# One image line loaded in two parts, a shorter second dummy product, and one warming instruction less, in an attention and gated feed-forward kernel

## The chip, the cores and the metric

The kernel runs on one core of a Trainium2 chip. The metric is the device time of one execution in microseconds (us). The engines are TensorE (PE in the profile; PEld is its weight load), VectorE (DVE), ScalarE (ACT), GpSimd (POOL) and SyncE (SP, which here only issues transfers). Sixteen DMA engines move the data; SP, ScalarE and GpSimd each have a queue of transfers that they issue (SPq, ACTq, POOLq).

## The reference

An attention over a pooled image, followed by a gated feed-forward layer. With four images (B = 4), 12288 queries for each, and 128 channels:

```
# q [4, 12288, 128], kv [4, 384, 32, 128], w_sr [128, 128]
kv_pool = kv.reshape(B, H // r, r, W // r, r, C).mean(axis=(2, 4))      # r = 4: 96 x 8 = 768 keys
k = v = kv_pool.reshape(B, -1, C) @ w_sr
a = softmax(q @ k.T / sqrt(C))
x = (a @ v).reshape(B * 12288, 128)
gate = maximum(x @ w_gate, 0.0)                                       # w_gate, w_val [128, 1536]
out = (gate * (x @ w_val)) @ w_out                                    # w_out [1536, 128]
```

All inputs and the output are float32.

## The kernel before

The queries are worked in 96 tiles of 512 rows (`T`), four to a group. For a tile, TensorE makes the scores against the 768 keys, ScalarE the exponentials, TensorE the weighted values, and then for each of twelve blocks of 128 hidden units a value product (line 504), a gate product (515) and, after VectorE has put the two together (523), an output product (545 or 529). The order in which all engines get these steps is written out by hand: a list of words `OPENING` for the first tiles, then `STEADY` for each tile, and `DRAIN` and `LAST` for the end. Each word is one step; `@n` behind it names the PSUM bank.

The change touches the very beginning. An image is pooled in six chunks of 128 keys. Two chunks are one pair, 128 image rows. `kv_load` brings a pair in as four "lines": line `dh` holds the rows `dh`, `dh`+4, `dh`+8 and so on. One line is a tile of 128 partitions with 1024 float32 each, 512 KB. Its source has 32 image rows ("hp"), and each row is cut into four pieces of 4 KB ("wp"), so that four neighbouring partitions hold one image row. For the first pair of the first image the lines go to two queues in turn:

```
kv_load(0, 0, range(r), (nc.sync, nc.scalar))
nc.sync.dma_start(w_sr_f32, w_sr)
q_load_pair(0)
q_load_pair(2)
kv_load(0, 1)
kv_load(0, 2)
```

So SP issues lines 0 and 2, then `w_sr` (line 642), two query pairs of 512 KB (line 181), and four lines each for the next two pairs (line 246; the last four are called `kv_line` in the profile). ScalarE issues lines 1 and 3, then loads its table, and runs two one-column exponentials, `warm` (line 651) and `spare` (652), whose results nothing reads.

TensorE begins with two dummy products, `fill(2)` (line 663), of the float32 identity matrix with a broadcast column of 512; their PSUM bank is given back at once. Then follows the start of `OPENING`:

```
T0.1@0 T1.1@1 T0.0 T1.0 T0.3 a1 T0.2 p1 kvT0 r1 cast0 pj0@0 T1.r cast1 qt0@2 key0 kvT1
```

- `Tj.d` (`turn_add`, line 300): four transposing matmuls that add the four pixel columns of line `d` of chunk `j` into a PSUM bank. The first one, `T0.1`, reads line 1.
- `a1`, `p1` and `r1` (line 272): chunk 1's lines 2 and 3 are added by VectorE, then the pixel columns by VectorE and GpSimd; `T1.r` transposes the result.
- `kvT0`, `kvT1` (line 143): VectorE copies the transposed chunk out of PSUM; `pj0` (line 314) multiplies it by `w_sr`, and `key0` (323) keeps the keys.
- `cast0`, `cast1`, `cast2` (line 141): ScalarE casts query tiles to float16 as soon as they have landed; `qt0` (line 209) transposes a tile on TensorE, `qT0` (143) copies it out, and `S` (378) are the scores.

The framework gives the transfers that SP and ScalarE issue eight semaphores in turn, in the order of the program. A transfer that takes a semaphore anew is issued only after the transfer that had it before, eight places back, has landed. The first such wait before the change stands at the second load of pair 1.

Of the kernel before, what the change touches and what calls it, by code (L numbers as in the profile page):

```python
# [11 lines left out]
AF = mybir.ActivationFunctionType  # L12
# [4 lines left out]
def kernel(  # L17
# [23 lines left out]
    nc = tc.nc  # L41

    B, N, C = q.shape
    _, H, W, _ = kv.shape
# [13 lines left out]
    X_SCALE = 512.0  # L58
    LEAD = GRP
    AT_BUFS = 4  # L60
    qk_scale = 1.0 / math.sqrt(C)

    assert C == 128 and N % T == 0 and J == 128 * NJC and D_FF == 128 * NFB
# [58 lines left out]
    def bank(shape, dtype=FP32):  # L122
        n = asked.pop() if asked else next(n for n in free_banks if n < usable[0])
        free_banks.remove(n)
        ps = pools[n // 6].tile(shape, dtype, tag=f"bank{n}", bufs=1, name="bank_ps")
        bank_numbers[id(ps)] = n, ps
        return ps
# [3 lines left out]
    def freed(ps):  # L131
        free_banks.append(bank_numbers.pop(id(ps))[0])
        return ps
# [95 lines left out]
    def kv_load(b, pair, lines=range(r), queues=(nc.sync,)):  # L229
        if (b, pair) not in kv_in:  # L230
            if (b, pair) == (0, NJC // 2 - 1):
                kv_in[b, pair] = [
                    work.tile([128, NS * J // 2], FP32, tag="a16", bufs=4, name="kv_line")[
                        :, 0 : 2 * r * C
                    ].rearrange("p (h dw c) -> p h dw c", h=2, dw=r)
                    for dh in range(r)
                ]
            else:
                lines_in = work.tile([128, r, 2, r, C], FP32, tag="kv_in", bufs=2, name="kv_in")
                kv_in[b, pair] = [lines_in[:, dh] for dh in range(r)]  # L240
        parts = kv_in[b, pair]
        rows = kv[b, pair * 2 * HC : (pair + 1) * 2 * HC].rearrange(
            "(hp dh) (wp h dw) c -> dh hp wp (h dw c)", dh=r, h=2, dw=r
        )
        for dh in lines:
            queues[dh % len(queues)].dma_start(  # L246
                parts[dh].rearrange("p h dw c -> p (h dw c)"), rows[dh]
            )

    s3s, kv_Ts, key_banks = {}, {}, {}  # L250

# [122 lines left out]
    def scores(k, jc):  # L374
        if k not in aTs:
            aTs[k] = work.tile([128, NJC, T], FP16, tag="aT", bufs=AT_BUFS, name="aT")
        s_ps = s_banks[k, jc] = bank([128, T])
# [9 lines left out]
    def score_block(k, s):  # L387
        b = k // NST
        if s == 0:
            a16s[k] = work.tile([128, NS, J], FP16, tag="a16", bufs=4, name="a16")  # L390
            aTs[k] = work.tile([128, NJC, T], FP16, tag="aT", bufs=AT_BUFS, name="aT")
            if k % 2 == 0:
# [238 lines left out]
    ident = const.tile([128, 128], FP32)  # L631
# [7 lines left out]

    w_sr_f32 = const.tile([128, C], FP32)  # L640
# [6 lines that stand above are left out]
    warm = const.tile([128, 1], FP32)  # L647
    spare = const.tile([128, 1], FP32)
    for tile_ in (spare, warm):
        nc.vector.memset(tile_, 0.0)  # L650
    nc.scalar.activation(warm, warm, AF.Exp)
    nc.scalar.activation(spare, spare, AF.Exp)

    wg16 = const.tile([128, D_FF], FP16)
    wv16 = const.tile([128, D_FF], FP16)
# [2 lines left out]

    idle = bank([128, 512])

    def fill(n):
        for _ in range(n):
            nc.tensor.matmul(
                idle, ident, ident[:, 0:1].to_broadcast([128, 512]), start=True, stop=True
            )

    fill(2)
    freed(idle)

    def fill_less(n):  # L670
# [135 lines left out]
    for word in OPENING:  # L806
        word, _, number = word.partition("@")
# [6 lines left out]
    for k in range(LEAD + 2, last + 1):  # L814
# [5 lines left out]
        b = k // NST + 1  # L820
# [3 lines left out]
        for word in words:  # L824
            head, n = word.rstrip("0123456789"), int(word.lstrip("abcdefghijklmnopqrstuvwxyzADPT") or 0)
# [29 lines left out]
            elif head in ("tb", "P", "pk"):  # L855
                pair, since = divmod(at - 6 if head == "tb" else at - 8, 4)
# [45 lines left out]
```

## Time and profile before

| | us |
|---|---|
| median of 3 runs | 1025.21 |
| lowest and highest | 1024.92, 1026.33 |
| the profiled execution | 1025.06 |
| its span, first to last instruction | 1023.3 |

| busy in the profiled span | us | share | instructions |
|---|---|---|---|
| TensorE matmul | 1016.5 | 99% | 5028 |
| TensorE weight load | 486.5 | 48% | 5028 |
| VectorE | 867.2 | 85% | 1447 |
| ScalarE | 918.3 | 90% | 1926 |
| GpSimd | 523.0 | 51% | 1311 |

The span is what the profiler saw of the instructions; the execution's own time is 1.76 us longer. A row of the timeline gives the start in us from the start of the span, the duration, the engine, the line of the kernel, the operation, what it writes and reads, how many instructions were merged, and in brackets the idle time before it with what ended it. A letter q behind an engine's name (SPq, ACTq) marks an instruction that issues a transfer; its duration is that of the issue, not of the transfer.

### The profile page before, as it was taken

The page shows a single profiled execution, that of the slowest core. Times are in us where ns is not written, and L with a number is a line of the kernel's source. Part 1 is how long each engine was busy: PE and PEld are TensorE (multiplying, and loading weights), DVE is VectorE, ACT ScalarE, POOL GpSimd, SP SyncE. Part 2 cuts the span into 40 slices and gives each one's busy share as a digit, 9 for nine tenths or more (in the row PEclk, how much of TensorE's full clock was granted, in tenths as well). Part 3 has the DMA queues.
Part 4 walks back from the last instruction along what each step waited for, and adds up shares of the span by engine and source line. Part 5 has one row for each costly group of instructions (what it writes and reads, how often), then busy time and mean ns, then how long its engine had stood idle before and what let it go on. Part 6 is the DMA issues. An engine that isn't in the chain of part 4 may idle for free.

```text
span 1023.3 us, 17491 instructions
## 1 busy us (share of the span) xinstructions
PE 1016.5 (99%) x5028; PEld 486.5 (48%) x5028; DVE 867.2 (85%) x1447; ACT 918.3 (90%) x1926; POOL 523.0 (51%) x1311
## 2 busy tenths in 40 slices
PE   8999999999999999999999999999999999999998
PEld 4444444444444444444444444444444444444445
DVE  4988888888888888888888888888888888888888
ACT  5999998999999999999999999989999999999986
POOL 3487857344347576544434856754434533443342
PEclk9999999999999999999999999999999999999999
DMA  9999998888799999768779989878777877777551
GB/s 316 167 170 184 194 201 146 140 126 125 139 196 157 199 168 181 137 116 144 124 132 204 172 172 196 159 125 137 128 132 113 147 122 129 124 119 124 98 91 44
DMA packets 475743, 153.48 MB, mean 150 GB/s; under 512 B 451584, under 2 KB 465920, under 8 KB 475648
## 3 DMA queue, kind: packets, MB, share of 16 engines
q1 hardware_dynamic: 453184, 126.08, 65.0%
q0 software_dynamic: 22032, 25.19, 18.0%
q10 hardware_dynamic: 432, 1.11, 0.3%
q8 instruction: 39, 0.64, 0.3%
q14 instruction: 56, 0.46, 0.2%
HBM read 53.94 MB, written 26.35 MB: 78 GB/s over the span
## 4 chain that ended last, share of the span: by engine, by line
PE 98%; DMA 1%; ACT 0%; SPq 0%; issue 0%
PE bank_ps L504 24%; PE bank_ps L515 24%; PE bank_ps L545 24%; PE wide_ps L397 12%; PE bank_ps L439 12%; DMA q<-in_q_dram 1%; PE bank_ps L529 1%; PE bank_ps L456 0%; PE bank_ps L378 0%; PE wide_ps L336 0%; PE bank_ps L300 0%; ACT aT L381 0%; PE bank_ps L314 0%; PE bank_ps L474 0%; SPq L246 0%
## 5 line engine op out<-in xcount | busy, mean ns | idle before, releaser
L523 DVE SCALAR_TENSOR_TENSOR hT<-bank_ps,val 128x512 f16<-128x512 f32 x1152 | 728.1, 680 | 104.5 <-PE bank_ps L515 83.8
L141 ACT CAST val<-bank_ps 128x512 f16<-128x512 f32 x1149 | 628.5, 596 | 44.6 <-PE bank_ps L504 24.2
L504 PE MATMUL bank_ps<-xT,wv 128*128 128x512 f16 x1152 | 420.6, 379 | 0.0
L515 PE MATMUL bank_ps<-xT,wg 128*128 128x512 f16 x1152 | 376.0, 379 | 0.0
L545 PE MATMUL bank_ps<-hT,wo 128*128 128x512 f16 x1116 | 348.5, 379 | 0.0
L402 ACT ACTIVATE a<-wide_ps 128x768 f16<-128x768 f32 x368 | 302.1, 821 | 44.1 <-PE wide_ps L397 44.1
L397 PE MATMUL wide_ps<-kv,qT 128*128 128x512 f16 x736 | 179.7, 326 | 0.0
L439 PE MATMUL bank_ps<-aT,kv 128*128 128x512 f16 x552 | 178.9, 379 | 0.0
L558 POOL TENSOR_TENSOR o_sb<-o_t,scale 128x512 f32<-128x512 f32 x89 | 93.2, 1047 | 159.6 <-issue 141.9
L545 PEld LDWEIGHTS <-wo 128*128 128x128 f16 x1116 | 109.2, 98 | 132.1 <-issue 1.1
L515 PEld LDWEIGHTS <-wg 128*128 128x128 f16 x1152 | 112.7, 98 | 122.6 <-issue 0.6
L504 PEld LDWEIGHTS <-wv 128*128 128x128 f16 x1152 | 112.6, 98 | 105.3 <-issue 0.6
L423 POOL COPY scale<-square 32x8 f32<-32x8 f32 x736 | 141.2, 192 | 28.6
L416 POOL TENSOR_TENSOR square<-inverse 128x8 f32<-128x8 f32 x46 | 9.3, 202 | 247.8 <-DVE inverse L414 241.0
L832 POOL DMA_DIRECT2D out_dram<-o_sb x208 | 130.3, 632 | 9.2 <-POOL o_sb L558 7.5
L397 PEld LDWEIGHTS <-qT 128*128 128x128 f16 x736 | 72.0, 98 | 86.9 <-issue 0.2
L447 DVE CAST xT<-bank_ps 128x512 f16<-128x512 f32 x92 | 63.6, 691 | 31.6 <-PE bank_ps L439 31.6
L439 PEld LDWEIGHTS <-kv 128*128 128x128 f16 x552 | 54.0, 98 | 65.2
L402 ACT ACTIVATION_READ_ACCUMULATOR a<-wide_ps 128x1 f32 x368 | 76.1, 207 | 0.0
L553 DVE STREAM_TRANSPOSE o_t<-bank_ps 128x512 f32<-128x512 f32 x93 | 65.4, 703 | 0.2 <-PE bank_ps L504 0.2
L162 POOL DMA_DIRECT2D q<-in_q_dram x84 | 48.8, 582 | 0.3 <-issue 0.3
L256 POOL TENSOR_TENSOR s<-kv_in 128x512 f32<-128x512 f32 x36 | 45.1, 1283 | 0.7
(81 smaller groups left out, 206.2 us busy)
## 6 DMA issues: line engine op xcount, KB each, us to landing
kv_in<-in_kv_dram SPq DMA_DIRECT2D x42, 512.0 KB, 5.2
out_dram<-o_sb SPq DMA_DIRECT2D x177, 64.0 KB, 3.6
q<-in_q_dram POOLq DMA_DIRECT2D x88, 128.0 KB, 3.5
out_dram<-o_sb POOLq DMA_DIRECT2D x176, 64.0 KB, 4.2
aT<-a SPq DMA_TRANSPOSE x184, 4.5
kv_line<-in_kv_dram SPq DMA_DIRECT2D x4, 512.0 KB, 9.9
placed<-blocks SPq DMA_DIRECT2D x9, 128.0 KB, 2.6
kvT<-placed SPq DMA_DIRECT2D x36, 32.0 KB, 2.2
```

The lines of the kernel that those rows point to most:

```text
L141: nc.scalar.copy(to, what)
L397: nc.tensor.matmul(s_ps[:, j0 * 128 : j1 * 128], qT, kv16[:, b, j0:j1, 0:C], start=True, stop=True)
L402: nc.scalar.activation(a16s[k][:, s, :], s_banks.pop(s)[:, 0:J], AF.Exp, scale=qk_scale, accum_out=a_sums[k // 2][:, k % 2, s : s + 1],)
L423: nc.gpsimd.tensor_copy(to[32 * b : 32 * (b + 1), :, :, j], squares[k // 2][32 * j : 32 * (j + 1)])
L439: nc.tensor.matmul(x_banks[k], kv16[:, k // NST, jc, C : 2 * C], aT[:, jc], start=first, stop=x_left[k] == 0,)
L504: nc.tensor.matmul(proj_banks["v", k, fb], wv16[:, fb * 128 : (fb + 1) * 128], xTs[k], start=True, stop=True,)
L515: nc.tensor.matmul(proj_banks["g", k, fb], wg16[:, fb * 128 : (fb + 1) * 128], xTs[k], start=True, stop=True,)
L523: nc.vector.scalar_tensor_tensor(hTs[k][:, fb, :], freed(proj_banks.pop(("g", k, fb))), 0.0, vals.pop((k, fb)), op0=ALU.max, op1=ALU.mult,)
L545: nc.tensor.matmul(o_banks[k], wo16[:, fb, :], hTs[k][:, fb, :], start=first, stop=o_left[k] == 0)
L553: nc.vector.transpose(o_t, freed(o_banks.pop(k)))
L558: nc.gpsimd.tensor_tensor(to, o_by, scale.to_broadcast([128, NS, 4, 32]), op=ALU.mult)
L832: queue.dma_start(*out_moves.pop())
```

## The change

Three edits. In `kv_load`, line 1 of the first pair of the first image is loaded by two transfers, partitions 0 to 31 (8 image rows) and 32 to 127 (24 image rows), both on ScalarE's queue, ahead of line 3. All other lines are loaded by one transfer as before. The tile and its readers stay the same; a reader of line 1 now waits for both. The exponential of `spare` is left out; its memset stays. The second dummy product has 384 columns instead of 512.

```diff
+    FIRST_CUTS = (0, 32, 128)
...
         for dh in lines:
-            queues[dh % len(queues)].dma_start(
-                parts[dh].rearrange("p h dw c -> p (h dw c)"), rows[dh]
-            )
+            cuts = FIRST_CUTS if (b, pair, dh) == (0, 0, 1) else (0, 128)
+            for p0, p1 in zip(cuts, cuts[1:]):
+                queues[dh % len(queues)].dma_start(
+                    parts[dh][p0:p1].rearrange("p h dw c -> p (h dw c)"), rows[dh, p0 // 4 : p1 // 4]
+                )
...
     nc.scalar.activation(warm, warm, AF.Exp)
-    nc.scalar.activation(spare, spare, AF.Exp)
...
-    def fill(n):
-        for _ in range(n):
-            nc.tensor.matmul(
-                idle, ident, ident[:, 0:1].to_broadcast([128, 512]), start=True, stop=True
-            )
-
-    fill(2)
+    for n in (512, 384):
+        nc.tensor.matmul(
+            idle[:, 0:n], ident, ident[:, 0:1].to_broadcast([128, n]), start=True, stop=True
+        )
     freed(idle)
```

In the program that results, TensorE, VectorE, GpSimd and SP have the same instructions in the same order; ScalarE has one more transfer in front and one activation less. The one more transfer moves the rotation of the eight semaphores on by one, so that each later transfer of SP's opening waits for another one than before: the first load of pair 1 for the first part of line 1, the next for line 0, then the second part of line 1, line 2, line 3, `w_sr`, and the two query pairs.

## The prediction

> **What bounds the kernel now.** I read the page first: the busy row (TensorE 99% of the span), then part 4, the chain that ended last.
>
> ```profile
> PE 98%; DMA 1%; ACT 0%; SPq 0%; issue 0%
> ```
>
> The one percent that is not TensorE sits at the start, where all three edits lie. The chain in order of time shows it: from 3.07 to 10.59 us the end of the kernel hangs on the load of the first query pair, then on its cast by ScalarE, then TensorE has the chain to the end.
>
> ```profile
> 3.07 7.53 DMA q<-in_q_dram
> 10.59 0.02 issue
> 10.62 1.15 ACT q L141 x2
> 11.77 0.05 issue
> 11.81 0.40 PE bank_ps L209 x4
> ```
>
> Next the timeline of the first 11 us (start, duration, engine, line, operation, shapes, and in brackets the idle time before it with its releaser).
>
> ```profile
> 0.74 1.56 SPq L246 DMA_DIRECT2D kv_in<-in_kv_dram  x2
> 0.74 1.29 ACTq L246 DMA_DIRECT2D kv_in<-in_kv_dram  x2
> 1.36 3.78 PE L663 MATMUL bank_ps<-ident 128*128 128x512 f32 x4 [1.36 <-POOL ident masks.py:199]
> 2.06 1.28 ACT L651 ACT_TABLE_LOAD   x1 [2.06 <-issue]
> 3.47 0.19 ACT L652 ACTIVATE spare<-spare 128x1 f32<-128x1 f32 x1
> 5.46 2.40 PE L300 MATMUL bank_ps<-ident,kv_in 128*128 128x128 f32 x16 [0.31 <-DMA kv_in<-in_kv_dram]
> 8.69 1.16 PE L300 MATMUL bank_ps<-ident,kv_in 128*128 128x128 f32 x8 [0.83 <-DMA kv_in<-in_kv_dram]
> 9.25 0.69 DVE L272 TENSOR_TENSOR kv_s<-kv_in 128x512 f32<-128x512 f32 x1 [8.34 <-DMA kv_in<-in_kv_dram]
> 10.62 1.90 ACT L141 CAST q<-q 128x512 f16<-128x512 f32 x3 [6.96 <-DMA q<-in_q_dram]
> 10.65 0.49 PE L314 MATMUL bank_ps<-kvT_chunk,w_sr_f 128*128 128x128 f32 x2 [0.81 <-DVE kvT_chunk L143]
> ```
>
> Every engine waits for loads. Last, busy time by microsecond (the last two columns are the DMA share and GB/s) and the queues between 2 and 4 us (q10 is ScalarE's, q1 SP's):
>
> ```profile
> 2.00:3.00 1.00, 1.00 (x2) 0.34 (x1) 0.00 (x0) 0.94 (x1) 0.08 (x1) 1.00 0.87 127
> 3.00:4.00 1.00, 1.00 (x2) 0.34 (x1) 0.00 (x0) 0.65 (x3) 0.00 (x0) 1.00 0.80 274
> 4.00:5.00 1.00, 1.00 (x2) 0.00 (x0) 0.00 (x0) 0.00 (x0) 0.00 (x0) 1.00 0.98 401
> 5.00:6.00 1.00, 0.69 (x4) 0.57 (x4) 0.00 (x0) 0.00 (x0) 0.00 (x0) 1.00 1.04 422
> ```
> ```profile
> q10 hardware_dynamic: 98, 0.40, 83.5%
> ```
>
> From 4 us on the DMA engines are full at some 410 GB/s, so a 512 KB load costs about 1.28 us of all sixteen engines (0.16 us for each of the 8 packets of 4 KB that fall to one engine). Until 4 us only line 1, ScalarE's first load, moves: no q1 packet is in that stretch, though SP issued line 0 at the same 0.74 us. Issue plus time to landing puts line 1 at 5.3, line 0 at 6.5, line 3 at 8.6, line 2 at 9.2, the first queries at 10.6: one behind the other, about 1.3 us for each 512 KB. So what counts in the opening is the total of the packets ahead of the first queries on the slowest DMA engine; who is first matters less.
>
> **The change, part by part.**
>
> *Warming activation removed.* ScalarE loses 0.19 us at 3.47 us and then waits until 10.62 us for the queries (6.96 us idle). Gain nothing. The extra issue on its queue, 0.62 to 0.64 us by the two rows of L246, pushes the table load from 2.06 to about 2.7 us and its end to 4.0; the remaining warming instruction ends near 4.2. The same 6.96 us hide that; without them it would cost 0.64 us less 0.19.
>
> *Shorter second dummy.* Each product runs as two passes; the passes start about 0.85 us apart (3.78 us for four with the tail). 384 of 512 columns take a quarter from two passes: 2 x 0.21 = 0.43 us, so the dummy ends near 4.72 instead of 5.14. TensorE already waits 0.31 us after it for line 1, so this gains nothing; it makes the wait longer. Its possible price is a clock that comes up later, below.
>
> *Semaphore rotation.* Transfers take eight semaphores in turn, and an issue waits for the transfer eight places back. One more transfer moves each wait of SP by one place: the first load of image pair 1, issued at 4.44 us without a wait, now waits for the 32-partition part; the three behind it for line 0, the 96-partition part and line 2; the first `kv_line` load for line 3. Queued behind on SP are only later image loads, then the late query tiles, which wait for GpSimd until 22.13 us. The readers of these loads are TensorE (waits of 0.41 and 0.34 us) and VectorE (0.65 and 0.40). The cover: the last of these issues stands at 11.89 us, while the load issued at 4.44 lands at 13.1, so q1 never runs dry. Cost nothing; with the cover gone, at most the 0.6 us of one issue.
>
> *The split.* The bytes are the same. Order changes: the 96-partition part is now ScalarE's second issue at about 1.4 us, where line 3 stood, and so comes behind line 0. Line 0 then has a quarter of line 1 before it and lands about 3/4 x 1.28 = 0.96 us earlier, near 5.5; the 96-partition part shares the engines with line 2 as line 3 did (between 5.6 and 8 us q1 had 53% and q10 50%), and needs 0.96 us alone or 1.9 us shared: line 1 is whole at 6.5 to 7.4 us instead of 5.3. Line 3 becomes the third issue and lands among the last, near the 9.2 us that line 2 had. TensorE's list has line 1 first, so its 16 transposes start at 6.5 to 7.4; at 0.11 us each, as the later ones of them run, they end by 9.2. The eight for lines 3 and 2 then follow at once and end near the 10.3 us at which VectorE copies their sum now. This is just hidden; if not, each 0.1 us of lateness is 0.1 us for the key chain, which has about 0.16 us of slack against the queries.
>
> What remains is how the two parts are spread over the sixteen engines. The loads of the trace have 32 blocks of four rows (one image row is four partitions), two whole blocks to an engine if they are spread evenly. The parts have 8 and 24 blocks. No row shows such a transfer. Lower bound: spread evenly, 2 and 6 packets, 0. Upper bound: a block stays whole, so 8 blocks fill at most eight engines with 4 packets each, and 24 blocks load some engines with 8 packets: 12 instead of 8, which is 4 x 0.16 = 0.64 us more on those engines for every later load. A gain on this term is excluded for the loaded engines, but if the engine that ends last now is one that is spared, part is won back. I take 0.5, near the end that keeps blocks whole, since all loads shown have whole numbers of blocks per engine.
>
> The Trainium skill, page "DMA: Bandwidth & Descriptors", section "Why a DMA increments its semaphore by 16 and not by 1", says that a copy runs on the largest number of engines, at most 16, that divides the slowest dimension of both sides. By that rule the parts run on 8 and 12 engines, and the sum would be the upper bound, 0.64 us; no run shown here has such a transfer, so the trace neither agrees nor disagrees.
>
> *Sum.* Warming 0, dummy 0, rotation 0, order 0, spread +0.5 us on the landing of the first queries. From there the chain is TensorE to the end, so it is passed on whole. The profiled execution took 1025.06 us, 1.76 more than its span of 1023.3; with 0.5 it becomes 1025.6. It lies 0.15 under the median of the runs shown, 1025.21, and against that the forecast is 1025.7.
>
> **The rivals.**
>
> *Evenly spread, order alone:* 0 to 0.2 us, 1025.3. For it: sixteen arrivals per load in all rows; against: 8 blocks are fewer than sixteen engines.
>
> *Earlier data:* the small part reaches the DMA engines sooner, and the slow first stretch (127 and 274 GB/s) is covered. At most the 0.43 us by which the dummy was shortened could be used: 1024.8. Against it: an issue costs 0.62 to 0.64 us here, and 0.33 to 0.38 at the kernel's end for small stores, so most of it is fixed; the second part comes a whole issue later.
>
> *A cold TensorE* (the one on the slower side). The transposes show two speeds:
>
> ```profile
> L300 PE MATMUL bank_ps<-ident,kv_in 128*128 128x128 f32 x4 | 1.1, 428 | 0.3 <-DMA kv_in<-in_kv_dram 0.3
> L300 PE MATMUL bank_ps<-ident,kv_in 128*128 128x128 f32 x13 | 1.7, 287 | 0.0
> ```
>
> The first row is from 5.4 to 6.3 us, the second from 6.45 to 8 us: 0.21 us from start to start, then 0.11. The step comes after about 5 us of nearly unbroken work. With the dummy ending at 4.72 and line 1 at 6.5 to 7.4 there is a hole of 1.8 to 2.7 us instead of 0.31. If the 0.11 us spacing comes only at about 9.8 us, 16 transposes cost up to 16 x 0.1 = 1.6 us more, of which the waits of 0.83 and 0.81 us absorb most: about +0.5 on top, 1026.2. If it comes only at 13 us, the 2.3 us of work between 10.65 and 13 double as well: 0.5 + 0.5 + 2.3 = 3.3, 1028.5. It decides where the 0.21 us spacing reaches past some 12 us. Against it: the hole is short beside the work after it. The Trainium skill, page "TensorE: Matmul & The Clock Gate", section "Part 1: The HAM clock gate (the "warmup" mystery)", has the clock follow a free-running window of 3.4 us; the step after some 5 us agrees, and by it a half-idle window would delay the fast clock by one window, the 1026.2 case.
>
> *No effect at all* would need the parts to be merged again; the order of instructions shows both on ScalarE's queue, so it has no chance of its own.
>
> **How the numbers follow.** Spread over fewer engines, +0.5: 0.45. Even: 0.24. Earlier data: 0.12. Cold to 9.8 us: 0.10. Cold to 13 us: 0.09. A measurement of this kernel can tell about 0.2%, 2.05 us, from no change: 1023.2 to 1027.3. Only the last case passes it; with 0.03 from the upper tail of the others slower has 0.12. Faster would need more than TensorE's waits of 0.31, 0.83 and 0.81 us together, so 0.03; same 0.85. The range runs from the earlier-data case with the low side of the runs (0.3 under the median) to above the cold-to-9.8 case with the high side (1.1 above the median): 1024.5 to 1027.2.
>
> **What would show it.** Right: three ScalarE issues at about 0.74, 1.4 and 2.0 us; the dummy at 3.35 us; the first transposes at 6.5 to 7.4; the cast of the queries at 11.1 instead of 10.62, and the products after it shifted by the same. Fewer engines: the two landings of line 1 and all later loads late by up to 0.64 us. Wrong: queries at 10.6 or earlier, or transposes at 0.21 us beyond 9.8 us, or any stage after 30 us that takes longer than before, for which I have no cause.

## The result, and the profile after

The changed kernel took 1030.8 us (median of 6 runs, 1030.54 to 1031.41) against 1025.45 for the kernel before (6 runs, 1024.92 to 1026.33): a ratio of 1.0053, 95% interval 1.0042 to 1.0063. It is slower by 5.35 us and lies outside the forecast range, on the side that had 0.12. The profiled execution took 1030.61 us with a span of 1028.8, 5.5 more than before.

The shares of the chain that ended last, on the page of the changed kernel:

```profile
PE 98%; DMA 1%; issue 0%; ACTq 0%; ACT 0%; DVE 0%
```

The loss is again in the one percent at the start. Against the trace of before, each TensorE instruction compared with the same one there, they are 5.6 to 6.8 us late from the first transposes on and 5.6 us late from 18.9 us (24.5 in the changed kernel) to the end. The chain in order of time (start, duration, what):

```profile
0.74 1.45 ACTq L249
2.19 0.03 issue
2.22 8.81 DMA kv_in<-in_kv_dram
11.03 0.14 issue
11.17 5.07 PE bank_ps L303 x24
16.24 0.02 issue
16.27 0.30 DVE kvT_chunk L144
16.57 0.04 issue
16.61 0.49 PE bank_ps L317 x2
```

Where the chain ran over the queries, it now runs over ScalarE's two issues, the second of which (the 96-partition part) is whole only at 11.03 us, and then over all 24 transposes in one piece. The timeline of the opening, to be laid beside that of before:

```profile
0.74 2.98 ACTq L249 DMA_DIRECT2D kv_in<-in_kv_dram  x3
0.74 1.33 SPq L249 DMA_DIRECT2D kv_in<-in_kv_dram  x2
1.36 3.35 PE L664 MATMUL bank_ps<-ident 128*128 128x512 f32 x4 [1.36 <-POOL ident masks.py:199]
3.75 1.28 ACT L654 ACT_TABLE_LOAD   x1 [3.75 <-issue]
11.17 5.06 PE L303 MATMUL bank_ps<-ident,kv_in 128*128 128x128 f32 x24 [6.45 <-DMA kv_in<-in_kv_dram]
12.12 1.14 ACT L142 CAST q<-q 128x512 f16<-128x512 f32 x2 [6.88 <-DMA q<-in_q_dram]
13.60 0.69 DVE L275 TENSOR_TENSOR kv_s<-kv_in 128x512 f32<-128x512 f32 x1 [12.69 <-DMA kv_in<-in_kv_dram]
16.61 0.49 PE L317 MATMUL bank_ps<-kvT_chunk,w_sr_f 128*128 128x128 f32 x2 [0.38 <-DVE kvT_chunk L144]
```

The dummy ends at 4.71 us, as forecast. Then TensorE waits 6.45 us instead of 0.31. The 24 transposes stand 0.21 us apart, all but the last two (5.06 us; before, 16 took 2.40 and 8 took 1.16). VectorE's sum of lines 2 and 3 comes at 13.60 instead of 9.25, since line 3 is whole only at 13.50. The first projection stands at 16.61 instead of 10.65.

The minimum, median and maximum duration in ns of ScalarE's three issues, from the answer on that line:

```profile
L249 ACTq DMA_DIRECT2D kv_in<-in_kv_dram x3: 652/821/1451, 0.7 to 3.1; - x3
```

In order they are 1451 (32 partitions), 821 (96) and 652 (line 3). The queues between 2 and 4 us, and the busy time by microsecond (last two columns DMA share and GB/s):

```profile
q1 hardware_dynamic: 94, 0.39, 84.6%
```
```profile
4.00:5.00 1.00, 0.72 (x2) 0.00 (x0) 0.00 (x0) 1.00 (x1) 0.00 (x0) 1.00 1.03 401
6.00:7.00 1.00, 0.00 (x0) 0.00 (x0) 0.00 (x0) 0.00 (x0) 0.00 (x0) 1.00 0.98 300
8.00:9.00 1.00, 0.00 (x0) 0.00 (x0) 0.00 (x0) 0.00 (x0) 0.00 (x0) 1.00 1.04 250
9.00:10.00 1.00, 0.00 (x0) 0.00 (x0) 0.00 (x0) 0.00 (x0) 0.00 (x0) 1.00 1.02 238
11.00:12.00 1.00, 0.83 (x4) 0.86 (x5) 0.00 (x0) 0.00 (x0) 0.00 (x0) 1.00 1.04 418
```

The order has turned round: before, q10 (ScalarE's) alone had packets up to 4 us; now q1 alone has. And from 6 to 11 us, while the 96-partition part moves, the engines are as full as ever (0.97 to 1.06) but move 238 to 307 GB/s. The packets show why: those of 4 KB, on both queues, take 256 to 283 ns on average between 7 and 10 us; before they took 159. At 11 us, when the part is done, the old rate is back. The first part, of 32 partitions, shows none of this: from 4 to 5 us, while its packets moved, they took 161 ns on average and the rate was 401 GB/s.

The landings in the two traces:

| whole at (us) | line 1 | line 0 | line 2 | line 3 | first queries | second queries |
|---|---|---|---|---|---|---|
| before | 5.32 | 6.58 | 9.15 | 8.64 | 10.59 | 11.87 |
| changed | 5.47 and 11.03 | 5.16 | 6.72 | 13.50 | 12.10 | 13.70 |

### The profile page after: what moved, and what is told of

Read it like the earlier page. It is cut to its first block, busy times and chain, and to the rows that moved or that the text cites. A ratio compares the mean times of both kernels' runs of the same rounds, so it can differ in the third digit from the quotient of the medians.

```text
span 1028.8 us, 17491 instructions
## 1 busy us (share of the span) xinstructions
PE 1017.4 (99%) x5028; PEld 488.4 (47%) x5028; DVE 867.2 (84%) x1447; ACT 918.2 (89%) x1925; POOL 522.9 (51%) x1311
## 4 chain that ended last, share of the span: by engine, by line
PE 98%; DMA 1%; issue 0%; ACTq 0%; ACT 0%; DVE 0%
PE bank_ps L507 24%; PE bank_ps L518 24%; PE bank_ps L548 23%; PE wide_ps L400 12%; PE bank_ps L442 12%; DMA kv_in<-in_kv_dram 1%; PE bank_ps L303 1%; PE bank_ps L532 1%; PE bank_ps L381 1%; PE bank_ps L459 1%; PE wide_ps L339 0%; PE bank_ps L317 0%; PE bank_ps L477 0%; ACTq L249 0%; PE bank_ps L210 0%
```

## The experiments

Diffs are against the changed kernel. Kernels were timed beside runs of the kernel before on the same chip, whose medians were 1024.88 to 1025.72; the ratio is to these. "First projection" is TensorE's first instruction of L317, "last line" the time at which the last of lines 0 to 3 is whole.

### Which of the three edits

**No split**, the two small edits alone.

```diff
-    FIRST_CUTS = (0, 32, 128)
+    FIRST_CUTS = (0, 128)
```

> Line 1 in one transfer again, with the shorter dummy and without the second warming instruction. If the split makes the loss (by its engines or by its place in the queue), this is the kernel before: within 1 us of it, line 1 landing at 5.3 us, the first transposes at 5.4. If the shorter dummy makes it (TensorE stays at its 0.21 us spacing), the loss stays: 2 to 5 us slower than before, transposes at 0.21 us well past 8 us.

1025.07 us, ratio 1.0004 (0.9994 to 1.0013). Line 1 is whole at 5.22 us again. The shorter dummy and the dropped warming instruction cost nothing that these runs can tell. The profiled execution, 1026.33 us, is 1.3 above the median. In it the clock, the column before the DMA share, was half from 11.12 to 14.54 us, with this opening too; TensorE was level with the trace of before until 11 us and 1.2 us late at what stood at 14 us there.

```profile
12.00:13.00 1.00, 1.00 (x7) 0.74 (x5) 1.00 (x5) 0.40 (x1) 0.00 (x0) 0.50 1.05 418
```

**Split only**, with the old dummy and both warming instructions.

```diff
+    nc.scalar.activation(spare, spare, AF.Exp)
-    for n in (512, 384):
+    for n in (512, 512):
```

> The split alone, both dummy products of 512 columns and both warming instructions. If the split makes the loss: 5 to 6 us slower than before, line 1 whole at about 11 us, 24 transposes at 0.21 us. If the dummy makes it: within 1 us of the kernel before.

1031.34 us, 1.0061 (1.0044 to 1.0078): the whole loss. The first issue took 1.46 us, the second part was whole at 11.03, line 3 at 13.49, and the first projection came at 16.90.

### Is it a second transfer, its size, or its partitions

**Two halves.**

```diff
-    FIRST_CUTS = (0, 32, 128)
+    FIRST_CUTS = (0, 64, 128)
```

> The changed kernel with the cut at 64 partitions: two parts of 16 source blocks each. If it is the number of engines that a part gets (8 and 12 with 8 and 24 blocks), both parts now run on all sixteen: 16 arrivals each, ScalarE's issues back to 0.6 to 0.7 us, the DMA rate above 400 GB/s from 4 us on, line 1 whole at 6 to 7.5 us, and the time 0 to 2 us above the kernel before. If any second transfer on ScalarE's queue falls behind SP's loads, line 1 stays late, at 9 us or more, and the loss is 3 to 5 us.

1026.0 us, 1.0011 (1.0001 to 1.002). Sixteen arrivals for each half. The issues are normal:

```profile
L249 ACTq DMA_DIRECT2D kv_in<-in_kv_dram x3: 608/618/665, 0.7 to 2.1; - x3
```

ScalarE's data come first again, and the halves are whole at 4.68 and 7.03 us. But the rate dips here too, to 291 and 303 GB/s between 5 and 7 us (packets of 0.21 to 0.26 us). The queries come 0.42 us later than before. The clock was half from 7.73 to 11.14 us in this execution, so the lost microsecond cannot be put down to the rate alone.

**A quarter, a quarter, a half**, so that no part has 96 partitions.

```diff
-    FIRST_CUTS = (0, 32, 128)
+    FIRST_CUTS = (0, 32, 64, 128)
```

> The changed kernel with line 1 in three parts of 32, 32 and 64 partitions: 8, 8 and 16 blocks, so no part has 24. If the part on twelve engines makes the slow stretch from 6 to 11 us (DMA engines fully busy at 250 to 300 GB/s), the rate is above 380 GB/s there and line 1 is whole at 7 to 9 us: 1 to 4 us slower than before. If parts on eight engines do it as well, or the number of transfers counts, it is as slow as the changed kernel or slower: 5 to 7 us.

1030.52 us, 1.0051 (1.0036 to 1.0066). Nearly all the loss without the 96-partition part: the first issue takes 1.457 us again, the second of the same size only 0.70; parts are whole at 5.64, 8.20 and 10.16, line 3 at 12.66. So the 12-engine part alone is not the cause. Here too the second part of 32 partitions moved with packets of 0.16 us (between 6 and 7 us), and packets were slow while the contiguous half moved (0.21 to 0.22 us between 8 and 10 us). Two other things differ here, and their share of the loss is not shown: one more transfer moves the rotation again (the second query pair is issued at 5.66 us instead of 3.40), and 22 of the 24 transposes ran 0.21 us apart.

**The larger part first.**

```diff
-    FIRST_CUTS = (0, 32, 128)
+    FIRST_CUTS = (0, 96, 128)
```

> Line 1 split into 96 and then 32 partitions, so the 12-engine part is issued first. If the issue's time goes with the number of engines (1.45 us for 8, 0.82 for 12): first issue 0.8 us, line 1's larger part is among the first packets and lands by 7 us, the smaller by 9 us, transposes start at 7 to 9 us: 1026.5 to 1029. If any transfer on fewer than 16 engines issues slowly when it is first: 1.45 us again, line 1 whole at about 11 us, 1030.5 to 1031. If the half clock were all of it, a start before 8.5 us would leave no more than 1.0 us of loss over the kernel with halves of 64 (1026.0).

1030.92 us, 1.0053 (1.0035 to 1.0072). The first issue takes 1.456 us with 12 arrivals as it did with 8, so its time does not go with the number of engines. The 96-partition part was whole at 7.69 us, yet from 8 to 10 us, with the last 32 partitions and other loads on their way, packets still took 0.23 to 0.26 us.

**The split on line 3**, ScalarE's second load.

```diff
-            cuts = FIRST_CUTS if (b, pair, dh) == (0, 0, 1) else (0, 128)
+            cuts = FIRST_CUTS if (b, pair, dh) == (0, 0, 3) else (0, 128)
```

> The same split in 32 and 96 partitions, on ScalarE's second load (line 3) instead of its first. Theory few engines (a transfer of 8 blocks issues slowly, and one of 24 blocks slows the packets beside it): ScalarE's first issue takes 0.64 us again and line 1 lands near 5.3; the DMA rate still falls below 320 GB/s while the 96-partition part moves, line 3 is whole at 10 to 13 us, and its eight last transposes put the first projection at 12.5 to 15: 1027 to 1029.5. Theory place (it is only that the slow first issue lets all of SP's loads go ahead): the rate stays near 410 GB/s, line 3 is whole by 9.7 us, 1025.0 to 1026.0. Theory any second transfer: as with two halves of 64, 1026.0.

1029.74 us, 1.0043 (1.003 to 1.0057), a little above the first theory's figure and far from the other two. Line 1 is issued in 0.68 us and whole at 6.42; now the second issue, the first of a part, takes 1.40. The rate falls to 168 GB/s between 8 and 9 us, line 3 is whole at 12.29, the first projection at 14.75. Where the parts stand matters less than that there are parts.

**The same bytes, cut along the row**: 256 and 768 elements of all 128 partitions.

```diff
-            cuts = FIRST_CUTS if (b, pair, dh) == (0, 0, 1) else (0, 128)
+            cuts = FIRST_CUTS if (b, pair, dh) == (0, 0, 1) else (0, 2 * r * C)
...
-                    parts[dh][p0:p1].rearrange("p h dw c -> p (h dw c)"), rows[dh, p0 // 4 : p1 // 4]
+                    parts[dh].rearrange("p h dw c -> p (h dw c)")[:, x0:x1], rows[dh, :, :, x0:x1]
```

with `FIRST_CUTS = (0, 256, 1024)`.

> The first line in two transfers of a quarter and three quarters of its bytes as in the changed kernel, but cut along the row: 256 and 768 of 1024 elements of all 128 partitions (packets of 1 and 3 KB). If any second transfer, or the size of the first, makes the loss: first issue 1.45 us, line 1 whole at 10 to 11 us, 1029 to 1031. If it is the partitions (a transfer that covers a part of them runs on fewer engines and makes packets slow): issues of 0.62 to 0.67 us, the rate stays near 410 GB/s, line 3 lands near 9.5 us, queries at 10.6 to 11.0: 1025.0 to 1026.2.

1025.75 us, 1.0007 (0.9998 to 1.0016): the loss is gone. Issues, rate and transposes of this kernel:

```profile
L249 ACTq DMA_DIRECT2D kv_in<-in_kv_dram x3: 622/625/642, 0.7 to 2.1; - x3
```
```profile
5.00:6.00 1.00, 0.47 (x2) 0.07 (x1) 0.00 (x0) 0.00 (x0) 0.00 (x0) 1.00 1.04 423
6.00:7.00 1.00, 0.65 (x3) 0.66 (x4) 0.00 (x0) 0.00 (x0) 0.00 (x0) 1.00 1.02 422
```

Line 1 is whole at 6.30 us, line 3 at 8.94, the queries at 10.30. This is nearly the opening that the prediction described, without its 0.5 us on the queries, and the kernel's time is that of before. Two transfers in the place of one, of a quarter and three quarters, cost nothing, and neither does the rotation, which is that of the changed kernel; the partitions do. Two transposes need the first part alone, and here they stand at 4.78 us, right behind the dummy.

**Even and odd partitions**, 64 each.

```diff
+            n = 2 if (b, pair, dh) == (0, 0, 1) else 1
+            for i in range(n):
+                    parts[dh][i::n].rearrange("p h dw c -> p (h dw c)"), rows[dh, :, i::n]
```

> The first line in two transfers of 64 partitions, as in the kernel with halves, but the even and then the odd ones, so that each spans the whole tile. If packets are slow because all engines write into one contiguous part of the partitions: packets stay at 0.16 us (0.24 to 0.26 with the contiguous halves), 410 GB/s, first queries at 10.6 instead of 11.0, 1024.9 to 1025.6. If two transfers in the place of one cost it: 1026.0 and 0.24 us packets as with the contiguous halves.

1025.68 us, 1.0004 (0.9995 to 1.0014), too near to the halves' 1026.0 to tell apart by time. The packets tell: 159 ns from 5 us on, 418 to 422 GB/s from 4 to 7 us, where the contiguous halves had 0.21 to 0.26 us. In its profiled execution the 24 transposes stood 0.21 us apart to the last, and the span (1024.6) is 1.3 us above that of before.

**120 and 8 partitions**, which covers nearly the whole tile.

```diff
-    FIRST_CUTS = (0, 32, 128)
+    FIRST_CUTS = (0, 120, 128)
```

> Line 1 cut into 120 and 8 partitions (30 and 2 blocks of four). By the rule of the greatest divisor: 15 and 2 arrivals. If fewer than sixteen engines is what costs (slow first issue, packets slowed on all engines): first issue 1.45 us, packets of 0.25 us or more and under 320 GB/s while the 120-partition part moves, line 3 at 12 us or later, 1028 to 1031. If it is that the parts cover a quarter or three quarters of the partitions: packets at 0.16 to 0.18 us, 400 GB/s, line 3 at 9.5 to 10.5 us, 1025.0 to 1026.5, whatever the first issue takes.

1030.17 us, 1.0047 (1.003 to 1.0064); 15 and 2 arrivals. The longest issue is the first:

```profile
L249 ACTq DMA_DIRECT2D kv_in<-in_kv_dram x3: 622/713/1540, 0.7 to 3.1; - x3
```
```profile
5.00:6.00 1.00, 0.00 (x0) 0.00 (x0) 0.00 (x0) 0.20 (x1) 0.00 (x0) 1.00 0.96 209
6.00:7.00 1.00, 0.00 (x0) 0.00 (x0) 0.00 (x0) 0.00 (x0) 0.00 (x0) 1.00 1.04 238
```

So a part need not be small: one that leaves out 8 partitions and one engine has the slow issue, and packets of 0.28 to 0.31 us between 5 and 7 us.

**Every fourth partition**, four transfers of 32 (the same edit with `n = 4`).

> The first line in four transfers of 32 partitions each, every fourth partition, so that each is as small as the first part of the changed kernel but has 32 blocks (one row of 4 KB each) spread over the whole tile, and 16 arrivals. If the number or the size of the transfers makes the loss: 1029 to 1032. If the loss needs contiguous partitions on fewer engines: issues of 0.62 to 0.67 us, packets near 0.16 us, line 3 behind five issues lands at 10 to 10.8 us, 1025.0 to 1027.0.

1031.52 us, 1.0063 (1.0046 to 1.0079), and yet not what the first theory says. Issues take 0.59 to 0.62 us, packets 159 ns, the rate is 395 to 425 GB/s from 5 to 8 us, line 1 is whole at 8.06 and the first queries at 9.14. But four transfers are two more in the rotation of eight semaphores, so ScalarE's issue of line 3 waits for line 0 and goes out at 5.51 us; line 3 is whole at 12.78:

```profile
8.20 3.65 PE L303 MATMUL bank_ps<-ident,kv_in 128*128 128x128 f32 x16 [3.48 <-DMA kv_in<-in_kv_dram]
12.82 1.97 PE L303 MATMUL bank_ps<-ident,kv_in 128*128 128x128 f32 x8 [0.98 <-DMA kv_in<-in_kv_dram]
15.17 0.80 PE L317 MATMUL bank_ps<-kvT_chunk,w_sr_f 128*128 128x128 f32 x2 [0.38 <-DVE kvT_chunk L144]
```

The test missed its aim, but shows another thing: at full rate and with early queries, one late line and transposes 0.21 us apart cost as much as the change does.

### How the 5.5 us divide

**Lines read as they land** (0, 2, 1, 3).

```diff
-        T0.1@0 T1.1@1 T0.0 T1.0 T0.3 a1 T0.2 p1 kvT0 ...
+        T0.0@0 T1.0@1 T0.2 T0.1 T1.1 T0.3 a1 p1 kvT0 ...
```

> The changed kernel with nothing altered but the order in which TensorE reads the four lines: as they land (0, 2, 1, 3) instead of 1, 0, 3, 2. If the 5.5 us are the wait for line 1 with 24 transposes behind it: lines 0 and 2 are turned from 5.3 us on, line 1's eight transposes end near 12.7 us, line 3 (13.5 us) is last with four, and the first projection stands at 14.0 to 14.8 us instead of 16.6: 1028.2 to 1029.0 us. If the later landing of the queries alone sets the loss (first pair 12.1 us instead of 10.6): 1030.8, as no query moves. If the engines lose it anywhere later than the opening: 1030.8 as well.

1030.74 us, 1.005 (1.0034 to 1.0066): no gain, though the first projection came at 15.19 instead of 16.61. In the profiled execution it was taken back at once, by the clock: TensorE was 4.5 us late at the projection, and 5.8 again by what stood at 13.5 us before.

```profile
12.00:13.00 1.00, 0.43 (x3) 0.09 (x1) 0.00 (x0) 1.00 (x2) 0.00 (x0) 0.54 1.02 406
15.00:16.00 1.00, 0.81 (x4) 0.75 (x5) 0.14 (x1) 0.00 (x0) 0.44 (x1) 0.50 1.02 406
17.00:18.00 1.00, 1.00 (x6) 0.66 (x5) 1.00 (x5) 0.00 (x0) 0.00 (x0) 0.50 1.05 418
```

The granted clock is half from 12.08 to 18.91 us, where work is dense; in the changed kernel full clock was recorded from 15.79 on.

**A longer dummy**, so that TensorE is busy until 10.5 us.

```diff
-    for n in (512, 384):
+    for n in (512, 384, 512, 512, 512, 512, 512):
```

> The changed kernel with five more dummy products of 512 columns, so that TensorE works through the hole until some 10 to 12 us and all data arrive as in the changed kernel. If the half clock costs what it seems to (24 transposes at 0.213 instead of 0.11 us, 2.5 us), the transposes run at 0.11 us, the last four wait for line 3 at 13.5 us, and the first projection comes at about 14.2 us instead of 16.6: 1028.3 to 1029.1. If the clock costs nothing because line 3 and the queries bound anyway: 1030.8. If the dummy overruns line 1's landing by a microsecond, up to 0.5 us of the gain is lost.

1029.75 us, 1.0042 (1.003 to 1.0055), below the changed kernel but with overlapping intervals, and above the range expected from the clock.

```profile
11.30 1.94 PE L303 MATMUL bank_ps<-ident,kv_in 128*128 128x128 f32 x16 [0.82 <-DMA kv_in<-in_kv_dram]
13.69 1.10 PE L303 MATMUL bank_ps<-ident,kv_in 128*128 128x128 f32 x8 [0.45 <-DMA kv_in<-in_kv_dram]
13.74 0.69 DVE L275 TENSOR_TENSOR kv_s<-kv_in 128x512 f32<-128x512 f32 x1 [12.84 <-DMA kv_in<-in_kv_dram]
15.17 0.49 PE L317 MATMUL bank_ps<-kvT_chunk,w_sr_f 128*128 128x128 f32 x2 [0.38 <-DVE kvT_chunk L144]
```

The transposes run at full clock as hoped (16 in 1.94 us), and then line 3 is late: whole at 13.66, projection 1.51 us after it. TensorE is 4.2 us late against the trace of before from 18 us to its last instruction, where the changed kernel is 5.6: the half clock is worth 1.4 us there, not the 2.5 expected, because line 3 stands right behind. The spans differ by 0.7 us only (1028.1 against 1028.8), as in this execution the time from the last store's issue to the end was 3.35 us and not 2.67; the medians differ by 1.05.

**Whole line 1, but ScalarE's data second on the engines**, with the warming instruction and its table load ahead of ScalarE's issues.

```diff
-    FIRST_CUTS = (0, 32, 128)
+    FIRST_CUTS = (0, 128)
...
+    nc.scalar.activation(warm, warm, AF.Exp)
     kv_load(0, 0, range(r), (nc.sync, nc.scalar))
```

(the lines that make `warm` go up with it)

> No split; ScalarE's warming instruction with its table load stands ahead of its two issues, so that line 1 is issued whole at some 2.4 us, where the changed kernel issues the 96-partition part (2.22), and line 3 at some 3.05 (3.07 there). Only the place in the queue is as in the changed kernel; every transfer has 128 partitions. If the place sets the loss (SP's loads go ahead while ScalarE's issues are late): line 1 whole at 9 to 11 us, line 3 near 11.5 to 12, transposes cold: 1028.5 to 1030.5. If the slow packets set it: the rate stays near 410 GB/s, line 1 lands at 7 to 8 us and line 3 at about 10.4, first projection at 11.5 to 12.5: 1025.5 to 1027.

1025.58 us, 1.0006 (0.9997 to 1.0015). The issue did not move as meant: it went out at 0.94 us, during the table load, and not at 2.4. That was enough to turn the order on the engines: between 3 and 4 us q1 has 78 packets and q10 one, as in the changed kernel. Line 1 is whole at 6.27, line 3 at 8.87, the queries at 10.26:

```profile
6.41 1.94 PE L303 MATMUL bank_ps<-ident,kv_in 128*128 128x128 f32 x16 [1.68 <-DMA kv_in<-in_kv_dram]
8.92 1.09 PE L303 MATMUL bank_ps<-ident,kv_in 128*128 128x128 f32 x8 [0.57 <-DMA kv_in<-in_kv_dram]
10.39 0.49 PE L317 MATMUL bank_ps<-kvT_chunk,w_sr_f 128*128 128x128 f32 x2 [0.38 <-DVE kvT_chunk L144]
```

So ScalarE's data second, by itself, costs nothing as long as the transfers are whole. A whole line issued as late as 2.22 us was not run.

**Line 3 on SP's queue** behind line 2, lines read in the order 0, 2, 3, 1; the two parts stay.

```diff
-        T0.1@0 T1.1@1 T0.0 T1.0 T0.3 a1 T0.2 p1 kvT0 ...
+        T0.0@0 T1.0@1 T0.2 T0.3 a1 p1 T0.1 T1.1 kvT0 ...
...
-                queues[dh % len(queues)].dma_start(
+                queues[dh % len(queues) * (dh < 3)].dma_start(
```

> The changed kernel's split, but line 3 goes on SP's queue behind line 2, so that ScalarE's queue carries only the two parts of line 1, and TensorE reads the lines in the order 0, 2, 3, 1. If the loss is that line 3 stands behind the slow parts in ScalarE's queue: lines 0, 2 and 3 land by 9 us, line 1 is the last at 10.5 to 11.2 us with eight transposes, the first projection comes at 12 to 13.3 us instead of 16.6, the queries at 12.1 us or a little later: 1026.5 to 1028.5. If the order of the queues does not matter, only the lost DMA rate and the half clock: 1029.5 to 1031.

1028.75 us, 1.0034 (1.0024 to 1.0044): 2 us better than the changed kernel, 0.25 above the expected range. Line 1 is whole at 11.42 (11.03 in the changed kernel), line 3 at 11.13 instead of 13.50. Line 3 was expected by 9; its sixteen arrivals spread over 3.8 us (7.30 to 11.13), where in the kernel with whole lines theirs spread over 0.65 (8.22 to 8.87). The rate was 210 to 231 GB/s between 8 and 11 us, and the clock half from 9.88 to 16.71.

```profile
11.17 2.82 PE L303 MATMUL bank_ps<-ident,kv_in 128*128 128x128 f32 x12 [3.71 <-DMA kv_in<-in_kv_dram]
13.79 0.64 PE L317 MATMUL bank_ps<-kvT_chunk,w_sr_f 128*128 128x128 f32 x2
```

Two things were changed at once here, the queue and the reading order; a new reading order without the queue (lines read as they land) gained nothing.

## Why the prediction was wrong

**Right at nothing:** the warming instruction, the shorter dummy and the rotation of semaphores. The kernel without the split took the time of before, and so did the row cut, which has the rotation of the changed kernel. SP's first load of pair 1 did wait for the 32-partition part (issued at 5.49 instead of 4.44 us), and the DMA engines stayed full, which is the cover that the prediction named. In the kernel with four transfers the rotation caught line 3, a load that counts, and that kernel lost as much as the changed one.

**The step that failed is "The split"**, the terms "order: 0" and "spread: +0.5".

- *Issues of 0.62 to 0.64 us.* The first issue of a transfer on fewer than sixteen engines took 1.40 to 1.54 us in every kernel that had one, whether with 8, 12 or 15 arrivals, a later one 0.70 to 0.84. No row of the trace of before bounded that. Together with the next issue it turned the order on the engines round; that order by itself, with whole lines, costs nothing (1025.58).
- *Line 1 whole at 6.5 to 7.4 us.* It was 11.03. The prediction let packets keep 0.16 us. Those of the first part did, but between 7 and 10 us, while the 96-partition part moved, packets took 0.26 to 0.28 on both queues. With the row cut, where packets kept 0.16 us, line 1 was whole at 6.30: the arithmetic of the order was sound, its price of a packet was not.
- *Line 3 near 9.2 us.* It was 13.50, and this is the term that carries the most. The prediction looked at the total ahead of the queries, but line 3 stands in ScalarE's queue behind the slow parts, while SP's loads, queries included, go by. The path itself was in the prediction, with the condition "this is just hidden; if not, each 0.1 us of lateness is 0.1 us for the key chain"; it was not hidden. Of the 4.86 us by which line 3 is late (13.50 against 8.64), 1.7 are the lost rate by an estimate: 273 GB/s on average from 6 to 11 us instead of 414 is 0.7 MB less. That is also about what the queries lost. The rest is place: before, line 3 landed ahead of the first queries, now behind them. At full clock the first projection follows the last line by 1.5 us: 9.15 and 10.65 before, 8.87 and 10.39 with whole lines, 13.66 and 15.17 with the longer dummy. So 13.50 - 9.15 = 4.35 us of lateness could not be hidden by anything. Line 3 taken out of that queue, with another reading order, gave 2 us back.
- *Spread +0.5.* That the parts would run on 8 and 12 engines was right: 8 and 12 arrivals followed one early jump of each semaphore. The first queries came 1.51 us later, not 0.5, since the bound priced 4 extra packets at 0.16 us and left out that all the others slow down. The Trainium skill, page "DMA: Bandwidth & Descriptors", section "Why a DMA increments its semaphore by 16 and not by 1", gives the number of engines by the largest divisor; the arrivals agree in every kernel (8, 12, 15, 2, and 16 for halves and whole lines). The section says nothing of the rate of the others, and the 0.64 us worked out from it was as wrong as the 0.5.

**The cold TensorE** was the right rival in kind, and under-weighted: it was given the 0.21 us spacing to 9.8 or 13 us and a hole of 1.8 to 2.7 us; the hole was 6.45 us and full clock was first recorded at 15.79. (The PEclk column stands at 1.00 before that first record; the spacing is the sign.) All 24 transposes cost 5.06 us; last line to projection took 3.11 us instead of 1.5, so 1.61 us on top of 4.35, which makes the 5.96 by which the projection is late; 0.3 of it is won back by 24 us. The longer dummy bears this out: with the clock kept at full, TensorE was 1.4 us less late, 4.2 us instead of 5.6, and those 4.2 are line 3's. The Trainium skill, page "TensorE: Matmul & The Clock Gate", section "Part 1: The HAM clock gate (the "warmup" mystery)", has the clock change at the ends of a free-running window of 3.4 us; the traces agree, with full and half stretches of 3.41 or 6.83 us at different places in each kernel (half from 7.73 to 11.14 with the halves, 12.08 to 18.91 where lines are read as they land).

**Open.** Why packets slow down is not settled. They did while parts of 96 and 120 partitions moved, on 12 and 15 engines, and less with contiguous halves on 16; they did not with row cuts, with even and odd partitions or with every fourth. But the parts of partitions 0 to 31 and, in the kernel with three parts, 32 to 63 moved at 0.16 us on 8 engines, while with partitions 96 to 127 on their way the packets took 0.23 to 0.26 us. So neither contiguous partitions nor few engines are enough by themselves; how engines and partitions meet in SBUF the traces do not show. Nor is it shown why only the first issue of a part is slow, nor how much of the loss that issue would make at full rate. No version here beats the kernel before; the row cut, the even and odd partitions and the whole line with ScalarE second match it.

## What to carry to other kernels

A load that is to come in pieces is cut along the row, with all 128 partitions in each piece: that kept 16 engines, 4 KB packets of 0.16 us and issues of 0.62 us, where cuts across contiguous partitions into unequal parts lost 0.4 to 0.6% of this kernel's time. For a chain that waits for several loads, follow each load through its own queue to its landing, and look at the last one; a sum over the bytes ahead of the queries hides a load that stands behind a slow neighbour. And a rival whose cause is a longer hole is to be worked out from the longest hole that the other unknowns allow, here 6.45 us and not 1.8 to 2.7.

## What was not expected of the hardware

- The first issue of a transfer on 8, 12 or 15 engines held ScalarE's queue for 1.40 to 1.54 us, later ones for 0.70 to 0.84; its issues of whole lines, halves, row cuts and strided cuts took 0.59 to 0.76.
- While a part on 12 or 15 engines moved, the DMA engines were full but fell to 168 to 307 GB/s instead of 410 to 420, and the packets of the other queue slowed as much as its own. The first part of 32 partitions, on 8 engines, moved at 401 GB/s.
- The clock fell to half for 3.41 or 6.83 us in the middle of the opening in several executions, with the halves (a wait of 2.58 us) as without a split (no wait above 1.06 us), and did not with whole lines and ScalarE second (a wait of 1.68 us); so the longest wait alone does not decide it. In the execution without a split it made TensorE 1.2 us late.
- A DMA issue placed behind an activation in ScalarE's list went out during its table load (at 0.94 us, while the load ran from 0.74 to 2.02).
